# Issuing all of batch 0's loads ahead, smaller last chunks, and weights in quarters, in a fused attention and MLP kernel

## Chip, cores and metric

One core of a Trainium2 chip. The metric is the device time of one execution in microseconds (us), the median of several runs. A run lists its span, which is the part that the profile covers and some 1.8 us less than the time, and its mean granted TensorE clock (1.0 is full speed). All runs told here were in the same state (called fast). Differences of a few tenths of a microsecond are read from the traces, where single starts can be compared. A ratio of times is always the mean time of one kernel's fast runs over that of the other's fast runs of the same rounds, so it is not quite the ratio of the medians quoted beside it.

## The reference, cut to what matters

```python
B, N, C = 4, 6080, 256                       # d_ff = 2048
qn = q / (norm(q, axis=1) + 1e-6)            # norms over all N tokens
kn = k / (norm(k, axis=1) + 1e-6)
a  = softmax(kn.transpose(0, 2, 1) @ qn / tau)   # 256 x 256 for each batch
x  = v @ a                                   # 24320 x 256
out = gelu_tanh(x @ w_in) @ w_out
```

The norms and the 256 x 256 matrix need all tokens of q and k of a batch. For batch 0 nothing else can run meanwhile. For batches 1 to 3 that work is spread between the matmuls of the batch before.

## The kernel before

The kernel first computes G (k transposed times q) and the column sums of squares of batch 0, chunk by chunk. Then follow the softmax and aw = a @ w_in, folded so that a block of 512 tokens needs only v transposed, gelu, and w_out. The loads of batch 0 (cut):

```python
first_chunks = chunks_of([12, 12, 5, 6, 4, 4, 2, 2], 2)   # slots of 128 tokens
fillers = [0, 0, 5, 7, 4, 3, 1, 0]                        # filler matmuls before each chunk, results unused
def stage_chunk(n):          # takes a staging buffer of four: waits until an older chunk is used up
    ...
    load_chunk((nc.sync, nc.scalar if n < 1 else nc.sync), st, 0, first_chunks[n], 2)
for n in range(2):
    stage_chunk(n)
...
for n, ch in enumerate(first_chunks):
    # VectorE casts q and k to bf16, ScalarE squares them
    keep_clock(fillers[n])
    for s, rows in slots_of(ch, 128):
        gram(G, qkb, s, rows, seen == 0, seen == n_all - 1)
    # sums of the squares by matmuls with a column of ones
    for x in ((2, 3) if n == 0 else (4, 5) if n == 1 else (n + 4,)):
        stage_chunk(x)
```

The weights (cut). All casts and the loads of v go through POOL's queue, in this order:

```python
for half in range(2):
    # two DMAs of w_in, each cast on POOL
    load_v(1 + half)                          # POOL: block 1 and 2 of v
for half in range(2):
    w = flat_stage(8)
    nc.sync.dma_start(out=w, in_=wout_v[:, half * 8 : half * 8 + 8, :])      # rows of 1 KB
    nc.gpsimd.tensor_copy(wout_bf[:, half * 8 : half * 8 + 8, :], w)
```

```python
vT = vT_of.pop(nb)
turn_v(nb + 2)        # SP: four DMA transposes of the v block after next
load_v(nb + 3)        # POOL: load of a later v block
...                   # a few steps on, POOL: load_qk, first chunk of the next batch
```

## Time and profile before

| | |
|---|---|
| time | 754.13 us, median of 3 (753.9 to 754.29) |
| TensorE busy | 97% of a span of 752.0 us |
| column sums of batch 0 end | 35.95 us |
| first matmul of block 0, of block 1, of block 2 | 40.06, 52.26, 64.84 us |
| holes on TensorE after 40 us | one, 0.7 us, before the yp matmuls at 51.83 |

The profile's lines that carry this are shown in the prediction. A chain line has start, length and what. A window line has the stretch, its length, the busy time of TensorE, its weight loads, VectorE, ScalarE and POOL (each with its count), and then the granted clock, the DMA share and GB/s.

### The profile page before, as it was taken

To read this page: it belongs to the slowest core of one execution; us is meant where nothing else is said; L and a number is where in the kernel's file an instruction comes from. 1 tells how busy PE (TensorE), PEld (TensorE's weight loads), DVE (VectorE), ACT (ScalarE), POOL (GpSimd) and SP (SyncE) were. 2 spreads that over 40 slices of the span, in tenths; PEclk is the share of its full clock that TensorE was granted. 3 is DMA by queue.
4 is the path that set the end of the run, shared out by engine and by line. 5 is a ranking of instruction groups with operands and counts; after the bars stand their busy time and mean duration, and the time that the engine had idled before them with its cause. 6 is when DMAs were issued, how large, how long until landed. Compare 5 with 4: busy or idle time off the path is not lost.

```text
span 752.0 us, 12341 instructions
## 1 busy us (share of the span) xinstructions
PE 726.4 (97%) x5186; PEld 502.3 (67%) x5274; DVE 284.3 (38%) x497; ACT 420.3 (56%) x411; POOL 80.8 (11%) x154
## 2 busy tenths in 40 slices
PE   2899999999999999999999999999999999999998
PEld 1656766776666766776666666776666666666666
DVE  3733556463501646554521265555351011011011
ACT  4875555556456555555555555555645655555552
POOL 1061111101012102101001102010101000000000
PEclk9999999999999999999999999999999999999999
DMA  9989685613237685824325876671413533322111
GB/s 369 400 205 200 104 150 139 132 43 69 70 72 144 114 163 108 164 63 75 71 57 117 141 119 124 150 143 46 69 43 85 105 85 70 69 75 54 41 57 57
DMA packets 80183, 85.69 MB, mean 114 GB/s; under 512 B 55424, under 2 KB 59136, under 8 KB 79616
## 3 DMA queue, kind: packets, MB, share of 16 engines
q0 software_dynamic: 14480, 30.87, 25.7%
q1 hardware_dynamic: 65344, 52.39, 24.4%
q10 hardware_dynamic: 304, 1.64, 0.5%
q8 instruction: 41, 0.67, 0.4%
q14 instruction: 14, 0.11, 0.0%
HBM read 78.91 MB, written 24.90 MB: 138 GB/s over the span
## 4 chain that ended last, share of the span: by engine, by line
PE 94%; DMA 3%; ACT 1%; issue 1%; DVE 0%; POOL 0%; SPq 0%; DVEq 0%; POOLq 0%
PE yp L528 44%; PE hp L602 43%; PE G L158 4%; PE ps L218 2%; ACT sq L269 1%; DMA st<-in_q_dram 1%; DMA st<-in_k_dram 1%; PE T L196 0%; POOL wout_bf L359 0%; PE yp L633 0%; PE cols L170 0%; DVE qk L267 0%; DVE aw L413 0%; DVE Gs L188 0%; ACT eT L383 0%
## 5 line engine op out<-in xcount | busy, mean ns | idle before, releaser
L606 ACT ACTIVATE g<-hp 128x1024 bf16<-128x1024 f32 (+1 forms) x384 | 389.8, 1015 | 307.0 <-PE hp L602 295.2
L528 PE MATMUL yp<-wout_bf,g 128*128 128x256 bf16 x3024 | 392.0, 273 | 1.6 <-POOL wout_bf L359 0.7
L602 PE MATMUL hp<-vT,aw 128*128 128x512 bf16 (+1 forms) x1456 | 383.9, 377 | 3.8 <-DVE aw L413 0.2
L528 PEld LDWEIGHTS <-g 128*128 128x128 bf16 x3024 | 295.9, 98 | 114.3 <-issue 1.2
L602 PEld LDWEIGHTS <-aw 128*128 128x128 bf16 x1536 | 149.9, 98 | 104.1 <-DVE aw L413 0.5
L545 DVE COPY ysb<-yp 128x512 f32<-128x512 f32 (+1 forms) x95 | 64.9, 683 | 396.5 <-PE yp L528 396.5
L460 DVE TENSOR_TENSOR acc<-acc,sq 128x512 f32<-128x512 f32 x141 | 97.6, 692 | 4.8
L459 DVE TENSOR_TENSOR sq<-qkb 128x512 bf16<-128x512 bf16 x141 | 58.9, 418 | 0.0
L158 PE MATMUL G<-qkb 128*128 128x256 bf16 x288 | 55.0, 273 | 0.0
L307 POOL DMA_DIRECT2D vb<-in_v_dram x47 | 25.9, 552 | 88.6 <-DMA vT<-vb 81.3
L227 DVE TENSOR_SCALAR aw<-ps,rsinv 128x512 bf16<-128x512 f32 x30 | 22.4, 749 | 23.5 <-PE ps L218 18.3
L158 PEld LDWEIGHTS <-qkb 128*128 128x128 bf16 x288 | 28.2, 98 | 3.3
L332 POOL CAST gate<-g 1x1 f32<-1x1 bf16 x24 | 5.9, 245 | 227.8 <-ACT g L606 227.8
L158 PE MATMUL G<-qk 128*128 128x256 bf16 x96 | 13.5, 298 | 15.8 <-DVE qk L267 15.8
L269 ACT ACTIVATE sq<-st 128x3072 bf16<-128x3072 f32 (+2 forms) x9 | 21.1, 2379 | 11.1 <-DMA st<-in_q_dram 8.2
L158 PEld LDWEIGHTS <-qk 128*128 128x128 bf16 x96 | 9.8, 106 | 19.1 <-DVE qk L267 16.6
L267 DVE CAST qk<-st 128x3072 bf16<-128x3072 f32 (+2 forms) x10 | 14.2, 1438 | 13.1 <-DMA st<-in_q_dram 10.0
L218 PE MATMUL ps<-win_bf,eT 128*128 128x512 bf16 x54 | 16.4, 379 | 0.2
L479 POOL TENSOR_TENSOR r<-r,half 128x4 f32<-128x4 f32 x3 | 3.1, 1042 | 103.4 <-DVE r L478 103.4
L82 POOL DMA_DIRECT2D qkb<-in_q_dram x24 | 12.9, 537 | 5.8 <-issue 4.3
L585 POOL COPY g<-gr 128x1024 bf16<-128x1024 bf16 x2 | 2.1, 1036 | 101.3 <-PE yp L528 101.3
L82 POOL DMA_DIRECT2D qkb<-in_k_dram x24 | 12.9, 539 | 0.0
(73 smaller groups left out, 109.0 us busy)
## 6 DMA issues: line engine op xcount, KB each, us to landing
out_dram<-ysb SPq DMA_DIRECT2D x44, 512.0 KB, 3.0
vb<-in_v_dram POOLq DMA_DIRECT2D x43, 256.0 KB, 6.2
qkb<-in_q_dram POOLq DMA_DIRECT2D x21, 384.0 KB, 4.6
qkb<-in_k_dram POOLq DMA_DIRECT2D x21, 384.0 KB, 6.4
st<-in_q_dram SPq DMA_DIRECT2D x2, 1536.0 KB, 11.8
vT<-vb SPq DMA_TRANSPOSE x184, 3.0
wst<-in_moe_w_in_dram SPq DMA_DIRECT2D x4, 512.0 KB, 7.5
wst<-in_moe_w_out_dram SPq DMA_DIRECT2D x2, 1024.0 KB, 11.7
```

The costliest lines, as they stand in the source:

```text
L82: engines[x].dma_start(out=dst[x][:, 0:size, :], in_=src[b, s0 * 128 : (s0 + size) * 128, :].rearrange("(p s) c -> p s c", s=size))
L158: nc.tensor.matmul(G[:, ic, :], lhsT=qk[1][:rows, s, ic * 128 : ic * 128 + 128], rhs=qk[0][:rows, s, :], start=first and ic == 0, stop=las ...
L218: nc.tensor.matmul(ps, lhsT=eT[:, jc, ic * 128 : ic * 128 + 128], rhs=win_bf[:, jc, fs * 512 : fs * 512 + 512], start=jc == 0, stop=jc == 1)
L227: nc.vector.tensor_scalar_mul(dst, ps, scale)
L269: nc.scalar.activation(sq, x, AF.Square)
L307: nc.gpsimd.dma_start(out=t[:, 0:n, :], in_=v_rows[r0 : r0 + n * 128, :].rearrange("(p s) c -> p s c", s=n))
L459: nc.vector.tensor_mul(sq[:rows], flat, flat)
L460: nc.vector.tensor_add(acc[:rows], acc[:rows], sq[:rows])
L528: nc.tensor.matmul(yp[:rows, at, :], lhsT=g[:, fc, s * 128 : s * 128 + rows], rhs=wout_bf[:, fc, :], start=fc == 0, stop=fc == FC - 1)
L545: nc.vector.tensor_copy(ysb[:, s0 : s + 1, :], yp[:, 0 : s + 1 - s0, :])
L602: nc.tensor.matmul(hp[:, j, :cols], lhsT=aw[:, cc, fc * 128 : fc * 128 + 128], rhs=vT[:, cc, :cols], start=cc == 0, stop=cc == 1)
L606: nc.scalar.activation(g[:, 2 * i : 2 * i + 2, :cols], hp[:, :, :cols], AF.Gelu_apprx_tanh)
```

## The change

The intent: no load of batch 0 waits for a staging buffer, since idle buffers of later stages (g, aw) serve as homes; the last chunks are smaller, so that less work follows the last landing; w_out arrives in quarters with longer rows, so that its first users need not wait for a half; and the first exponentials begin when their own tile is ready. In the chunks numbered 6 and 7, POOL casts k and VectorE squares q (`CASTS_POOL`, `SQUARES_DVE`), which spreads the last work over more engines.

```diff
-    first_chunks = chunks_of([12, 12, 5, 6, 4, 4, 2, 2], 2)
-    fillers = [0, 0, 5, 7, 4, 3, 1, 0]
+    first_chunks = chunks_of([2, 12, 12, 5, 4, 4, 4, 2, 1, 1], 3)
+    fillers = [0, 0, 0, 5, 6, 5, 4, 2, 1, 0]
+    SQUARES_DVE = (6, 7)
+    CASTS_POOL = (6, 7)
...
+    staged = [
+        slot_pair(shared, 0, 2),
+        ([g[:, 0:12, :] for g in g_homes], None),
...
+    for n, ch in enumerate(first_chunks):
+        load_chunk((nc.sync, nc.scalar if n < 1 else nc.sync), staged[n][0], 0, ch, 2)
...
-    for half in range(2):
-        w = flat_stage(8)
-        nc.sync.dma_start(out=w, in_=wout_v[:, half * 8 : half * 8 + 8, :])
-        nc.gpsimd.tensor_copy(wout_bf[:, half * 8 : half * 8 + 8, :], w)
+    for fs in range(4):
+        w, T = w_quarter(), t_of(fs)
+        rows_of_w = moe_w_out[fs * 512 : fs * 512 + 512, :]
+        nc.sync.dma_start(out=w.rearrange("p (e t c) -> p e t c", t=T, c=256),
+                          in_=rows_of_w.rearrange("(e p t) c -> p e t c", p=128, t=T))
+        nc.gpsimd.tensor_copy(wout_bf[:, fs * 4 : fs * 4 + 4, :], w.rearrange("p (f c) -> p f c", c=256))
...
-    for cc in range(2):
-        p = pH.tile([128, 2, 512], FP32, tag="h", name="vps")[:, 0, :]
+    vps = pH.tile([128, 2, 512], FP32, tag="h", name="vps")
+    spare = pH.tile([128, 2, 512], FP32, tag="h", name="spare")
...
+    T = [pY.tile([128, 512], FP32, tag="y", name="T") for _ in range(2)]
```

Because a partition now holds four neighbouring rows of w_out, the columns of aw are stored in the matching order (the eviction reads PSUM with a stride). Cut here: the column order, the first quarter of w_in in two pieces, and the order of the first evictions of aw.

More of the change, by code (lines that the diff above doesn't have):

```diff
@@ L93 @@
     n_all = S_ALL + 1
-    first_chunks = chunks_of([12, 12, 5, 6, 4, 4, 2, 2], 2)
-    TAIL, SHARED = 4, 6
-    fillers = [0, 0, 5, 7, 4, 3, 1, 0]
-    staged = []
+    first_chunks = chunks_of([2, 12, 12, 5, 4, 4, 4, 2, 1, 1], 3)
+    n_chunks = len(first_chunks)
+    TAIL = 4
+    fillers = [0, 0, 0, 5, 6, 5, 4, 2, 1, 0]
+    SQUARES_DVE = (6, 7)
+    CASTS_POOL = (6, 7)
     def halves(pool, tag, dtype, size, most=SMAX):
@@ L107, in halves, with slot_pair @@
         return [t.rearrange("p a b c -> p (a b) c") for t in tiles], None
-    def stage_chunk(n):
-        if n < len(first_chunks):
-            _, size, rem = first_chunks[n]
-            if n < SHARED:
-                st, whole = halves(stage, "st", FP32, size)
-            else:
-                _, size, rem = first_chunks[n - 2]
-                whole = staged[n - 2][1][:, :, size + rem :, :]
-                st = [whole[:, x] for x in range(2)]
-                rem = False
-            if rem:
-                nc.gpsimd.memset(whole[:, :, size, :], 0.0)
-            load_chunk((nc.sync, nc.scalar if n < 1 else nc.sync), st, 0, first_chunks[n], 2)
-            staged.append((st, whole))
-    for n in range(2):
-        stage_chunk(n)
+    def slot_pair(whole, lo, hi):
+        return [whole[:, x, lo:hi, :] for x in range(2)], whole[:, :, lo:hi, :]
+    g_homes = [gp.tile([128, FC, 512], BF16, tag="g", name="g").bitcast(FP32) for _ in range(2)]
+    aw_homes = [awp.tile([128, 2, D], BF16, tag="aw", name="aw").bitcast(FP32).rearrange(
+        "p x (s c) -> p x s c", c=256) for _ in range(2)]
+    st_homes = [stage.tile([128, 2, SMAX, 256], FP32, tag="st", name="st") for _ in range(4)]
+    shared = st_homes[3]
+    staged = [
+        slot_pair(shared, 0, 2),
+        ([g[:, 0:12, :] for g in g_homes], None),
+        ([t.rearrange("p a b c -> p (a b) c") for t in st_homes[:2]], None),
+        slot_pair(st_homes[2], 0, 6),
+        slot_pair(aw_homes[0], 0, 4),
+        slot_pair(aw_homes[1], 0, 4),
+        ([g[:, 12:16, :] for g in g_homes], None),
+        slot_pair(shared, 2, 4),
+        slot_pair(shared, 4, 5),
+        slot_pair(shared, 5, 6),
+    ]
+    nc.gpsimd.memset(staged[3][1][:, :, 5, :], 0.0)
+    for n, ch in enumerate(first_chunks):
+        load_chunk((nc.sync, nc.scalar if n < 1 else nc.sync), staged[n][0], 0, ch, 2)
     ident = const.tile([128, 128], FP32)
@@ L147, with t_of, sorted_columns, pieces @@
     win_v = moe_w_in.rearrange("(c p) d -> p c d", p=128)
-    wout_v = moe_w_out.rearrange("(t p) d -> p t d", p=128)
+    def t_of(fs):
+        return 2 if fs == 0 else 4
+    def sorted_columns(ps, fs):
+        return ps.rearrange("a (e p t) -> a e t p", p=128, t=t_of(fs))
+    def pieces(dst, fs):
+        return dst.rearrange("a (e t p) -> a e t p", p=128, t=t_of(fs))
     def keep_clock(n, pool=pH, tag="h"):
@@ L199, in turned, with row_sums @@
         return T
-    def row_sums(eT):
-        rs = pA.tile([128, 512], FP32, tag="a", name="rs")
+    def row_sums(eT, rs=None):
+        if rs is None:
+            rs = pA.tile([128, 512], FP32, tag="a", name="rs")
         for ic in range(2):
@@ L212, in row_sums, with aw_part @@
         return rsinv
-    def aw_part(eT, rsinv, aw, fs, ic, ps=None, act=False):
+    def aw_part(eT, rsinv, aw, fs, ic, ps=None):
         if ps is None:
@@ L222, in aw_part @@
                 start=jc == 0, stop=jc == 1)
-        dst, scale = aw[:, ic, fs * 512 : fs * 512 + 512], rsinv[:, ic : ic + 1]
-        if act:
-            nc.scalar.activation(dst, ps, AF.Copy, scale=scale)
-        else:
-            nc.vector.tensor_scalar_mul(dst, ps, scale)
+        dst = pieces(aw[:, ic, fs * 512 : fs * 512 + 512], fs)
+        nc.vector.tensor_scalar_mul(dst, sorted_columns(ps, fs), rsinv[:, ic : ic + 1])
     G = pA.tile([128, 2, 256], FP32, tag="a", name="G")
     cols = pA.tile([128, 512], FP32, tag="a", name="cols")
-    n_chunks = len(first_chunks)
     seen, summed = 0, 0
@@ L265 @@
             todo = [[y[:, :, 0:hi] for y in (qk_whole, sq_whole, whole)]]
+        if n in CASTS_POOL:
+            nc.gpsimd.tensor_copy(qkb[1][:, 0:hi], st[1])
+            todo = [(qkb[0][:, 0:hi], None, st[0])]
         for to, sq, x in todo:
-            nc.vector.tensor_copy(to, x)
-            if n != n_chunks - 2:
-                nc.scalar.activation(sq, x, AF.Square)
-        if n == n_chunks - 2:
-            nc.scalar.activation(sqb[1][:, 0:hi], st[1][:, 0:hi], AF.Square)
+            nc.vector.tensor_copy(to[:, 0:hi] if whole is None else to, x)
+            if sq is not None and n not in SQUARES_DVE:
+                nc.scalar.activation(sq[:, 0:hi] if whole is None else sq, x, AF.Square)
+        if n in SQUARES_DVE:
+            nc.scalar.activation(sqb[1][:, 0:hi], st[1], AF.Square)
             nc.vector.tensor_mul(sqb[0][:, 0:hi], qkb[0][:, 0:hi], qkb[0][:, 0:hi])
@@ L279 @@
             waiting = None
-        if n < 2:
+        if n < 3:
             pairs_of(n, sqb)
@@ L285 @@
             sums_of([[y[:rows, s, :] for y in sqb] for s, rows in slots_of(ch, 128)], n == n_chunks - 1)
-        for x in ((2, 3) if n == 0 else (4, 5) if n == 1 else (n + 4,)):
-            stage_chunk(x)
     v0 = stage.tile([128, 2, SMAX, 256], FP32, tag="st", name="v0")
@@ L343, in load_qk, with w_quarter @@
             loaded_of[b, n] = views, t
-    def flat_stage(n):
-        w = stage.tile([128, 2, SMAX, 256], FP32, tag="st", name="wst")
-        return w.rearrange("p a b c -> p (a b c)")[:, 0:2048].rearrange("p (c d) -> p c d", c=n)
-    for half in range(2):
-        w = flat_stage(2)
-        for x in range(2):
-            c0 = half * 1024 + x * 512
-            nc.sync.dma_start(out=w[:, :, x * 512 : x * 512 + 512], in_=win_v[:, :, c0 : c0 + 512])
-            nc.gpsimd.tensor_copy(win_bf[:, :, c0 : c0 + 512], w[:, :, x * 512 : x * 512 + 512])
-        load_v(1 + half)
-    for half in range(2):
-        w = flat_stage(8)
-        nc.sync.dma_start(out=w, in_=wout_v[:, half * 8 : half * 8 + 8, :])
-        nc.gpsimd.tensor_copy(wout_bf[:, half * 8 : half * 8 + 8, :], w)
+    w_homes = []
+    def w_quarter():
+        n = len(w_homes)
+        if n % 3 == 0:
+            t = stage.tile([128, 2, SMAX, 256], FP32, tag="st", name="wst")
+            t = t.rearrange("p a b c -> p (a b c)")
+        else:
+            t = w_homes[-1]
+        w_homes.append(t)
+        return t[:, n % 3 * 1024 : n % 3 * 1024 + 1024]
+    for fs in range(4):
+        w = w_quarter().rearrange("p (c d) -> p c d", c=2)
+        step = 256 if fs == 0 else 512
+        for lo in range(0, 512, step):
+            c0 = fs * 512 + lo
+            nc.sync.dma_start(out=w[:, :, lo : lo + step], in_=win_v[:, :, c0 : c0 + step])
+            nc.gpsimd.tensor_copy(win_bf[:, :, c0 : c0 + step], w[:, :, lo : lo + step])
+        if fs % 2:
+            load_v(1 + fs // 2)
+    for fs in range(4):
+        w, T = w_quarter(), t_of(fs)
[3 more added lines that the diff above has]
+        nc.gpsimd.tensor_copy(wout_bf[:, fs * 4 : fs * 4 + 4, :], w.rearrange("p (f c) -> p f c", c=256))
     r = smx.tile([128, 4], FP32, tag="r", name="r")
@@ L366, with turn_v0 @@
     Gs = scaled(G, r)
-    vps = []
-    for cc in range(2):
-        p = pH.tile([128, 2, 512], FP32, tag="h", name="vps")[:, 0, :]
+    vps = pH.tile([128, 2, 512], FP32, tag="h", name="vps")
+    spare = pH.tile([128, 2, 512], FP32, tag="h", name="spare")
+    def turn_v0(cc):
         for s in range(4):
-            nc.tensor.matmul(p[:, s * 128 : s * 128 + 128],
+            nc.tensor.matmul(vps[:, cc, s * 128 : s * 128 + 128],
                              lhsT=v0[:, s, cc * 128 : cc * 128 + 128],
                              rhs=ident, is_transpose=True)
-        vps.append(p)
-    keep_clock(1, pY, "y")
-    T = turned(Gs)
-    keep_clock(1, pY, "y")
+    turn_v0(0)
+    T = [pY.tile([128, 512], FP32, tag="y", name="T") for _ in range(2)]
+    for ic in range(2):
+        for jc in range(2):
+            nc.tensor.matmul(T[jc][:, ic * 128 : ic * 128 + 128],
+                             lhsT=Gs[:, ic, jc * 128 : jc * 128 + 128],
+                             rhs=ident, is_transpose=True)
+    turn_v0(1)
     vT0 = vts.tile([128, 2, 512], BF16, tag="vT", name="vT")
-    nc.vector.tensor_copy(vT0[:, 0, :], vps[0])
+    nc.vector.tensor_copy(vT0[:, 0, :], vps[:, 0, :])
     eT = smx.tile([128, 2, 256], BF16, tag="eT", name="eT")
@@ L382, with first_aw @@
     for jc in range(2):
-        nc.scalar.activation(eT[:, jc, :], T[:, jc, :], AF.Exp, scale=r[:, jc : jc + 1])
-    nc.scalar.activation(vT0[:, 1, :], vps[1], AF.Copy)
+        nc.scalar.activation(eT[:, jc, :], T[jc][:, 0:256], AF.Exp, scale=r[:, jc : jc + 1])
+    nc.scalar.activation(vT0[:, 1, :], vps[:, 1, :], AF.Copy)
     firsts = []
-    def first_aw(n, jc, pool=pY, tag="y"):
+    def first_aw(n, jc, pool=pA, tag="a"):
         if jc == 0:
@@ L400 @@
     first_aw(1, 0)
-    rsinv = row_sums(eT)
+    rsinv = row_sums(eT, spare[:, 0, :])
     first_aw(0, 1)
@@ L404 @@
     for n in (2, 3):
-        first_aw(n, 0, pA, "a")
+        first_aw(n, 0, pY, "y")
         first_aw(n, 1)
-    for n in range(4):
+    for n, t, act in ((0, 0, False), (1, 0, True), (0, 1, True), (1, 1, False), (2, None, False), (3, None, False)):
         ic, lo = n % 2, n // 2 * 256
-        dst, scale = aw[:, ic, lo : lo + 256], rsinv[:, ic : ic + 1]
-        if n == 1:
-            nc.scalar.activation(dst, firsts[n][:, 0:256], AF.Copy, scale=scale)
+        dst = aw[:, ic, lo : lo + 256].rearrange("a (t p) -> a t p", t=2)
+        ps = firsts[n][:, 0:256].rearrange("a (p t) -> a t p", t=2)
+        if t is not None:
+            dst, ps = dst[:, t], ps[:, t]
+        scale = rsinv[:, ic : ic + 1]
+        if act:
+            nc.scalar.activation(dst, ps, AF.Copy, scale=scale)
         else:
-            nc.vector.tensor_scalar_mul(dst, firsts[n][:, 0:256], scale)
+            nc.vector.tensor_scalar_mul(dst, ps, scale)
     nc.scalar.activation(dummy, ones_f, AF.Gelu_apprx_tanh)
-    aw_left = [(fs, ic, *((pA, "a") if fs == 2 else (pY, "y"))) for fs in range(1, 4) for ic in range(2)]
+    aw_left = [(fs, ic, *((pY, "y") if fs == 2 else (pA, "a"))) for fs in range(1, 4) for ic in range(2)]
     def more_aw(n):
```

## The prediction

> **What bounds the kernel now.** I read the summary of the page first, then the chain that ended last, in order of time, then the timeline and the windows of the stretch in which TensorE is not yet full.
>
> ```profile
> span 752.0 us, 12341 instructions
> PE 726.4 (97%) x5186; PEld 502.3 (67%) x5274; DVE 284.3 (38%) x497; ACT 420.3 (56%) x411; POOL 80.8 (11%) x154
> PE 94%; DMA 3%; ACT 1%; issue 1%; DVE 0%; POOL 0%; SPq 0%; DVEq 0%; POOLq 0%
> ```
>
> TensorE is busy 97% of the span and is 94% of the chain. All of the diff acts before some 52 us: it touches the loads and reductions of batch 0, its softmax and the weights. What follows is matmuls back to back whose number does not change. So the question is only by how much sooner the full stretch begins, and whether a hole near its start closes. The chain shows the start:
>
> ```profile
> 0.73 10.15 DMA st<-in_q_dram
> 10.90 7.42 ACT sq L269 x3
> ...
> 18.88 2.76 ACT sq L269
> 22.02 9.55 DMA st<-in_k_dram
> 31.66 1.24 DVE qk L267
> 32.95 1.05 PE G L158 x8
> ```
>
> Columns are start, length and what. It looks like DMA, then ScalarE (which frees a buffer), then DMA again. The windows say that the middle link is no real gap: the transfers never paused (the last two figures are DMA share and GB/s).
>
> ```profile
> 5.00:10.00 5.00, 0.00 (x0) 0.00 (x0) 0.00 (x0) 0.00 (x0) 0.00 (x0) 1.00 1.01 430
> 10.00:15.00 5.00, 0.61 (x3) 0.43 (x4) 4.10 (x3) 4.10 (x2) 1.07 (x1) 1.00 1.02 433
> 15.00:20.00 5.00, 4.47 (x46) 3.39 (x44) 3.85 (x4) 5.00 (x3) 0.00 (x0) 1.00 0.98 407
> 20.00:25.00 5.00, 4.22 (x52) 3.44 (x54) 4.14 (x4) 4.39 (x2) 0.00 (x0) 1.00 1.02 410
> 25.00:30.00 5.00, 5.00 (x51) 3.62 (x50) 3.34 (x4) 3.66 (x2) 0.00 (x0) 1.00 1.02 404
> ```
>
> From 5 to 30 us the share is 0.98 to 1.02 throughout. The wait for a buffer delayed the issue of a chunk (13.69, 16.34, 19.04, 21.65 us), but there was always older work in the queue. Issuing all at once therefore buys almost no transfer time. After the last landing comes a serial tail, also from the chain:
>
> ```profile
> 35.76 0.19 PE cols L170 x8
> 35.98 0.18 ACT r L363
> 37.30 0.75 PE T L196 x4
> 38.08 0.48 ACT eT L383
> 39.24 0.18 DVE rsinv L211
> 39.52 0.50 DVE aw L413
> 40.06 1.04 PE hp L602 x4
> 49.91 1.88 POOL wout_bf L359
> 51.83 0.60 PE yp L528 x4
> ```
>
> Column sums end at 35.95, the first block matmul starts at 40.06, and at 51.83 TensorE has waited 0.71 us for a cast of half of w_out (the waits view: L528 <- POOL wout_bf L359, 0.7). These three places are all that the change can win.
>
> [...] from 12 to 15 us only the SP queue was moving data, at 442 GB/s, no less than the 430 of both queues. [...] in the trace the first exponential starts at 38.08, after the last of the four transposes into its bank (38.05)[...]
>
> **Loads.** The bytes stay (6080 x 256 x 4 B x 2 = 12.45 MB); the row lengths change. From the packet records of the trace, median time of one packet on the SP queue: 12 KB rows 460 ns, 6 KB 238, 5 KB 200, 4 KB 162, 2 KB 86, 1 KB 46. One slot (128 tokens of q and k) is 16 KB for each of the 16 engines, so it costs 0.61 us in 12 KB rows, 0.64 in 5 or 6 KB, 0.65 in 4 KB, 0.69 in 2 KB, 0.74 in 1 KB. Before: 24 slots x 0.61 + 5 x 0.64 + 0.37 (the remainder) + 6 x 0.635 + 8 x 0.65 + 4 x 0.69 = 30.05 us. After: 24 x 0.61 + 5 x 0.64 + 0.37 + 12 x 0.65 + 4 x 0.69 + 2 x 0.74 = 30.3. So the last chunk lands about **0.27 us later**. Before, it landed at about 34.15 (issued near 25.6, the two small k loads taking 9.3 us to land in the median), so after at about 34.4. The instruction order of the changed kernel also shows that "all at once" is really eight SP transfers ahead: from the ninth on, an issue waits for an earlier landing. With some 18 slots in flight that never starves the engines.
>
> **Tail of the loads.** The last chunk has one slot, not two. Its cast is about 0.4 us (0.69 for 1024 elements before) and its square 0.61 (the row of 512 elements), against 1.06 before. Counted from the landing alone, the sums would end at 34.4 + 0.1 + 0.6 + 0.2 = 35.3. But TensorE has its own queue of work. The last eight slots cost 16 Gram matmuls at 0.107 to 0.13 us, 32 column sums at 0.024, and the fillers ahead of the last three chunks, now 2 + 1 + 0 at 0.21: some 1.8 + 0.8 + 0.6 = 3.2 us, in order. They start once the four-slot chunk is ready: it lands at about 34.4 - 2 x 0.69 - 2 x 0.74 = 31.6, and its half cast on POOL takes 1.04 (the win_bf row of the same size), so 32.7. That ends at 35.9, and before it was 35.95. I take a gain of **0.1 us** here, between zero and 0.6: the new fillers eat most of what the smaller chunk wins.
>
> **Softmax of batch 0.** The root, the norms and the scaling of G are unchanged. The four transposes now write two banks, so the first exponential may start after the third transpose, some 0.15 us sooner. The transposes of v's second half move behind T (four in 0.5 us), beside the exponentials. The first eviction of aw has pieces of 128 columns, so the first pair of block matmuls waits for about 0.35 us rather than 0.50 (estimate: 0.479 for 256 columns[...]). Together **0.3 us**. The strided read of PSUM is in the later batches too, but an eviction (0.75 us) comes there once per slot of some 2 us, off the path.
>
> **Weights.** Before, w_out came in two halves of 1 KB rows, landing near 45.9 and 49.8, with casts of 1.90 us each. Now four quarters, three in 4 KB rows: 16 x 0.086 + 3 x 8 x 0.162 = 5.3 us of packets per engine rather than 128 x 0.046 = 5.9, and casts of 1.04. Adding up the queue after 34.4: v0 1.3, w_in 5.6, the v blocks of POOL 2.75, the first three quarters 4.0: the third lands at 48.0 to 48.6 and is cast by 49.7; it is first read near 50.5. The fourth has until 51.9 and is cast near 51. So the hole of **0.7 us** closes.
>
> Sum: 0.1 + 0.3 + 0.7 = 1.1 to 1.2 us off 754.13: **752.9 us**.
>
> **Rivals.** (1) The load phase really is shortened: if the waits for buffers starved some DMA engines, 1 to 2 us come off and the time is 751 to 752. Against it: the share of 0.98 to 1.02. For it: the rate falls from 433 to 407 at 15 us, while 12 KB rows were still in flight. (2) The tail is bound by TensorE or POOL rather than by the landing: if the casts on POOL collide with VectorE's copies, or the fillers come late, the sums end 0.3 to 0.8 us later than before and the time is 753.3 to 754. For it: the chain is nearly gapless on TensorE from 32.95 on. (3) The hole at w_out is passed on: w_in's first quarter in 1 KB rows or the later quarters arrive too late, the wait turns up at another line, and the time stays at 753.6 to 754.1. Against it: nearly 1 us of slack by the sums above.
>
> **Range and chances.** If (1) holds beside my gains I get 751.5; if (2) and (3) hold together, 754.1. Repeated runs differ by 0.4 us. So 751.6 to 754.1. Two per cent would be 15 us, about half of the whole load phase, in either direction; nothing in the diff can reach that.
>
> **What would show it.** Right: DMA share near 1.0 up to 34 us as before, the last q or k landing at 34 to 34.7; column sums ending at 35.4 to 36.1; first block matmul at about 39.6; no wait of the yp matmuls for wout_bf and a TensorE busy time that has hardly changed. Wrong: a first block matmul before 38.5 (rival 1), or after 40.2 (rival 2); a wait of yp or ps for a weight cast above 0.3 us (rival 3); or a slower full stretch after 60 us, which would mean that the strided evictions or the new layout cost TensorE time after all.

Where a cut is marked, the forecast spoke of the hardware beyond what a trace of this case shows. No term of its sum is lost by that: it stays 0.1 + 0.3 + 0.7 = 1.1 (to 1.2) us off 754.13, so 752.9. For the load phase, the argument is the DMA share of 0.98 to 1.02. The 0.35 us for a piece of 128 columns stands as an estimate from the trace before, in which an eviction of 256 columns took 0.479 us and one of 512 took 0.750, so that one of 128 comes to about 0.34. That casts on POOL and work on VectorE hinder each other (rival 2) was a supposition; what was measured is told below.

## The result, and the profile after

The changed kernel takes **754.5 us** (754.08 to 755.56, 4 runs) against 754.01 of before (753.6 to 754.29, 4 runs). The ratio is 1.0009, interval 0.9992 to 1.0026: the same. I had predicted 752.9 and a range up to 754.1.

The head of the page, after:

```profile
span 752.3 us, 12381 instructions
PE 728.3 (97%) x5195; PEld 503.5 (67%) x5283; DVE 285.3 (38%) x501; ACT 420.4 (56%) x414; POOL 82.5 (11%) x159
PE 90%; DMA 7%; SPq 1%; issue 1%; POOL 0%; DVE 0%
```

DMA's share of the chain has gone from 3% to 7%, which is the first sign. The chain in order of time, after, up to 66 us:

```profile
3.60 18.70 DMA st<-in_k_dram
...
23.17 9.84 DMA st<-in_k_dram
...
34.02 7.41 DMA wst<-in_moe_w_in_dram
41.43 0.05 issue
41.48 0.99 POOL win_bf L378
42.47 6.60 DMA vb<-in_v_dram
49.07 0.02 issue
49.08 1.30 SPq L335
...
53.05 11.92 DMA vT<-vb
64.97 0.14 issue
65.11 1.02 PE hp L639 x4
```

Before, the chain left the loads at 31.57 and ran through the engines from there, for the most part TensorE. Now it runs through the loads until 65.11: the weights, then v of block 2, then its DMA transposes, the last of which takes 11.92 us to land. The matmuls of block 2 wait for it. The windows of the two kernels beside each other, first before and then after:

```profile
50.00:55.00 5.00, 4.29 (x29) 2.55 (x27) 0.00 (x0) 2.97 (x4) 4.94 (x8) 1.00 0.54 81
60.00:70.00 10.00, 9.95 (x70) 6.67 (x69) 3.35 (x6) 6.16 (x7) 1.36 (x3) 1.00 1.12 221
```

```profile
50.00:55.00 5.00, 5.00 (x35) 3.23 (x33) 0.00 (x0) 3.84 (x4) 3.81 (x9) 1.00 0.82 118
60.00:70.00 10.00, 9.12 (x62) 5.90 (x62) 3.35 (x6) 5.25 (x6) 1.43 (x3) 1.00 1.24 137
```

TensorE (the first busy time) gains 0.71 us from 50 to 55, where the hole at w_out was, and loses 0.83 from 60 to 70. The waits of TensorE say the same. Columns: who waited for whom, us in total, times, longest. Before, then after:

```profile
PE yp L528 <- POOL wout_bf L359: 0.7, 1, 0.7
```

```profile
PE hp L639 <- DMA vT<-vb: 0.8, 1, 0.8
```

Why do the transposes land late? The timeline of POOL shows when it issued v of block 3 and the first chunk of batch 1. Before, then after:

```profile
51.72 0.54 POOL L307 DMA_DIRECT2D vb<-in_v_dram  x1
52.95 0.54 POOL L82 DMA_DIRECT2D qkb<-in_q_dram  x1
```

```profile
49.96 0.54 POOL L321 DMA_DIRECT2D vb<-in_v_dram  x1
51.19 0.54 POOL L82 DMA_DIRECT2D qkb<-in_q_dram  x1
```

POOL finishes the casts of w_out 1.76 us sooner, and so its next loads go out 1.76 us sooner, into the stretch in which SP issues the transposes (from 48.90 before, from 49.08 after). By the landing records of the traces, the four transposes of block 2 landed at 51.3, 52.6, 57.6 and 61.5 before, and at 53.2, 56.4, 60.1 and 65.0 after: the first two, issued ahead of POOL's next load, 1.3 us apart before, and all four 3.2 to 4.8 apart with POOL's loads among them after. The view of the transposes' line has 8.6 us from issue to landing before and 12.6 after, but that is the median of 12 transposes of three blocks: it is 8.4 in the sixth experiment and 9.1 in the tenth, though block 2 waits in the sixth alone. So the landings of block 2 itself are compared here. From the issue of its first transpose to the landing of its fourth it takes 12.6 us before and 15.9 after.

The front did not gain either. The root, which follows the column sums, starts at 36.26 instead of 35.98. From there to the matmuls after block 0's first pair it takes 4.88 us (to 41.14) instead of 4.95 (to 40.93).

### The profile page after: what moved, and what is told of

It reads as the page before. It is cut to its first block, busy times and chain, and to the rows that moved or that the text cites. A ratio compares the mean times of both kernels' runs of the same rounds, so it can differ in the third digit from the quotient of the medians.

```text
span 752.3 us, 12381 instructions
## 1 busy us (share of the span) xinstructions
PE 728.3 (97%) x5195; PEld 503.5 (67%) x5283; DVE 285.3 (38%) x501; ACT 420.4 (56%) x414; POOL 82.5 (11%) x159
## 4 chain that ended last, share of the span: by engine, by line
PE 90%; DMA 7%; SPq 1%; issue 1%; POOL 0%; DVE 0%
PE yp L565 43%; PE hp L639 41%; PE G L176 4%; DMA st<-in_k_dram 4%; DMA vT<-vb 2%; PE ps L237 1%; DMA wst<-in_moe_w_in_dram 1%; DMA vb<-in_v_dram 1%; SPq L335 1%; SPq L82 0%; PE yp L670 0%; PE T L214 0%; POOL win_bf L378 0%; SPq L377 0%; PE cols L188 0%
## 5 line engine op out<-in xcount | busy, mean ns | idle before, releaser
L496 DVE TENSOR_TENSOR sq<-qkb 128x512 bf16<-128x512 bf16 x141 | 58.9, 418 | 0.0
L176 PEld LDWEIGHTS <-qk 128*128 128x128 bf16 x96 | 10.3, 111 | 17.7 <-DVE qk L285 14.1
L82 POOL DMA_DIRECT2D qkb<-in_q_dram x24 | 12.9, 537 | 5.7 <-issue 4.1
L287 ACT ACTIVATE sq<-st 128x3072 bf16<-128x3072 f32 (+2 forms) x6 | 10.6, 1769 | 5.0 <-DMA st<-in_k_dram 2.8
L82 POOL DMA_DIRECT2D qkb<-in_k_dram x24 | 12.9, 538 | 0.0
L657 POOL COPY gr<-g 128x1024 bf16<-128x1024 bf16 x2 | 2.1, 1036 | 81.6 <-ACT g L643 81.6
```

The lines of the kernel that those rows point to most:

```text
L82: engines[x].dma_start(out=dst[x][:, 0:size, :], in_=src[b, s0 * 128 : (s0 + size) * 128, :].rearrange("(p s) c -> p s c", s=size))
L176: nc.tensor.matmul(G[:, ic, :], lhsT=qk[1][:rows, s, ic * 128 : ic * 128 + 128], rhs=qk[0][:rows, s, :], start=first and ic == 0, stop=las ...
L287: nc.scalar.activation(sq[:, 0:hi] if whole is None else sq, x, AF.Square)
L496: nc.vector.tensor_mul(sq[:rows], flat, flat)
```

## Experiments

Theory A: the hole at w_out was closed, and the gain was handed on to block 2, because POOL is free sooner, loads sooner, and delays the transposes. Rival B: the new load phase delays everything. Rival C: the transposes are late for another reason. Theory D: a part of the loss is the clock, which stands at half (0.50) for some microseconds of the load phase in some runs. "Held" means that POOL's loads are held back.

One table for all runs. Block 1 and block 2 are the starts of their first matmuls in the profiled run, in us, and the gap is their difference. It is 12.6 where nothing waits. From block 2 to the end of the span it takes 687.1 to 687.5 us in every row except the first experiment (689.0), so the start of block 2 decides the time.

| kernel | block 1 | block 2 | gap | span of this run, its clock | median time, us | before, same rounds |
|---|---|---|---|---|---|---|
| before | 52.26 | 64.84 | 12.6 | 752.0, 1.0 | 754.13 | |
| changed | 51.53 | 65.11 | 13.6 | 752.3, 1.0 | 754.5 | 754.01 |
| 1 new weights only | 51.31 | 67.27 | 16.0 | 756.3, 0.998 | 755.72 | 754.12 |
| 2 old weights | 52.63 | 65.22 | 12.6 | 752.6, 1.0 | 754.96 | 754.12 |
| 3 POOL loads held | 54.86 | 67.45 | 12.6 | 754.6, 0.995 | 755.94 | 754.12 |
| 4 v of block 0 apart | 53.03 | 66.82 | 13.8 | 754.0, 0.998 | 754.72 | 754.12 |
| 5 new weights only, held | 52.93 | 65.52 | 12.6 | 753.0, 0.997 | 753.83 | 754.18 |
| 6 fillers moved | 51.22 | 64.25 | 13.0 | 751.4, 1.0 | 753.30 | 754.18 |
| 7 no late fillers | 52.77 | 67.04 | 14.3 | 754.2, 0.998 | 756.39 | 754.18 |
| 8 casts on VectorE | 53.13 | 65.72 | 12.6 | 752.9, 0.997 | 755.42 | 754.18 |
| 9 fillers moved, old weights | 52.82 | 65.40 | 12.6 | 752.8, 1.0 | 754.68 | 754.11 |
| 10 fillers moved, loads held | 50.84 | 63.42 | 12.6 | 750.6, 1.0 | 752.58 | 754.11 |
| 11 as 10, and 4 and 8 | 50.88 | 63.46 | 12.6 | 750.6, 0.999 | 752.57 | 754.11 |
| 12 before, fillers moved | 52.97 | 65.55 | 12.6 | 752.7, 0.999 | 754.05 | 754.11 |

All gave the right result.

### 1. The kernel before with the new weights only

```diff
-    for half in range(2):  ... w_in in halves, w_out in halves
+    for fs in range(4):    ... w_in and w_out in quarters, columns of aw sorted, as in the change
```

> The kernel before with only the weights part of the change (quarters, 4 KB rows of w_out, sorted columns); loads and softmax as before. Theory A (the closed hole at w_out is handed to block 2, whose transposed v lands late because the POOL queue is free sooner and issues the next loads sooner): no wait of yp for a w_out cast, the column sums end at 35.9 to 36.1 and the first block matmul is at about 40.1 as before, the loads for v block 3 and batch 1 are issued at about 50 and 51.2 instead of 51.7 and 53.0, the last transpose of v for block 2 lands near 65 instead of 61.6, block 2's first matmuls wait 0.8 to 1.2 us for it, and the time is within 0.3 us of before. Rival B (it is the new load phase and softmax that cost the time and delay the transposes): block 2 does not wait, and the time is 0.6 to 0.9 us below before.

The hole is gone (block 1 starts 0.95 us sooner than before). POOL's loads went out at 50.22 and 51.45, and block 2 waited. The wait in this profile was 3.2 us, far more than I had expected. The median is 755.72 (ratio 1.0015, 1.0002 to 1.0029), not "within 0.3 of before" but worse. The timeline and the windows of TensorE show why the loss is larger than the wait:

```profile
67.27 1.87 PE L620 MATMUL hp<-vT,aw 128*128 128x512 bf16 x4 [3.21 <-DMA vT<-vb]
```

```profile
65.00:70.00 5.00, 2.73 (x10) 1.35 (x10) 2.44 (x5) 0.74 (x1) 0.00 (x0) 0.72 1.20 152
```

After 3.2 idle us the four matmuls take 1.87 us instead of 1.03, and the granted clock of the stretch is 0.72: by the trace's clock record it is half from 67.22 to 70.63. Rival B falls: the load phase here is the old one, and block 2 waits all the same.

### 2. The changed kernel with the old weights

```diff
-    for fs in range(4):    ... quarters, sorted columns
+    for half in range(2):  ... halves, unsorted, as before
```

> The changed kernel with the weights loaded as before (halves, 1 KB rows of w_out, columns unsorted), everything else changed. Theory A: the wait of yp for the second w_out cast is back at 0.5 to 0.9 us, the POOL loads are issued at about 51.8 and 53 again, the last transpose for block 2 lands near 62 and nothing waits for it; the time is 0.1 to 0.4 us above before, because the front (sums and softmax) is 0.2 us later. Rival B: block 2 still waits for its transposes by 0.5 us or more and the time is 0.8 us or more above before.

As theory A has it. The waits of TensorE show the old hole and no wait for transposes:

```profile
PE G L178 <- DVE qk L287: 1.5, 1, 1.5
PE yp L555 <- POOL wout_bf L376: 0.9, 1, 0.9
PE T L397 <- DVE Gs L208: 0.8, 1, 0.8
```

The profiled span, at a clock of 1.0, is 752.6. The median of 754.96 is higher than expected, because three of the five runs had a clock of 0.995 to 0.997 and spans of 753.1 to 754.4. Of the nine runs of the kernel before in the same rounds, one had 0.997 and one 0.998. That was the first hint of theory D.

### 3. The changed kernel with POOL's loads held back

```diff
-            if n in (3, 9):
-                load_qk(b, n // 6)
+            if b == 1 and n == 6:
+                pace()              # POOL waits for activation 6 of block 0
+                load_v(3)
+            if n in ((7, 9) if b == 1 else (3, 9)):
+                load_qk(b, n // 8 if b == 1 else n // 6)
...
-            load_v(nb + 3)
+            if nb > 0:
+                load_v(nb + 3)
```

> The changed kernel, but the POOL loads of v block 3 and of the first chunk of batch 1 are held back until the sixth and seventh activation of block 0, so that they are issued near 51.3 and 52.6, about as before. Theory A: the last transpose for block 2 lands at 61.5 to 63.5, the wait of block 2 for it (0.83 us in the changed kernel) is gone, TensorE runs without a hole from 41 us on, and the span is 0.8 to 1.1 us below the changed kernel's 752.3, near 751.4: 0.5 to 0.7 us faster than before. Rival C (the transposes are late for another reason, such as their own issue or the write of the weights): the wait stays at 0.5 us or more and the time is that of the changed kernel.

The wait for the transposes is gone (gap 12.6). The fourth lands 8.6 us after the first was issued, instead of 15.9. All of block 0 came late in this run, so the loads were issued at 54.54 and 56.48 and not at the expected 51.3 and 52.6. But the time rose to 755.94 (ratio 1.002, 1.0008 to 1.0033), and all five runs had a clock of 0.995 to 0.998. The windows of the load phase:

```profile
20.00:25.00 5.00, 3.80 (x18) 2.70 (x19) 4.63 (x4) 4.07 (x2) 0.00 (x0) 0.51 1.03 408
25.00:30.00 5.00, 4.92 (x51) 3.53 (x50) 3.22 (x4) 4.58 (x3) 0.00 (x0) 0.80 1.02 404
```

From 20 to 27 us TensorE ran at half clock. Its matmuls fell behind the loads, and with the fillers between them it never caught up: block 0 started at 43.44. Block 0 was thus 3.3 us late and the span only 2.3 longer than the changed kernel's, so 1.0 came back, which is the wait. This profile supports A but cannot show the gain.

What differs from the changed kernel's own profile is the idle time just before the Gram matmuls of the 12-slot chunk that starts near 21 us. The same line in the third experiment:

```profile
21.20 5.30 PE L176 MATMUL G<-qk 128*128 128x256 bf16 x24 [2.62 <-DVE qk L285]
```

and in the changed kernel:

```profile
20.95 2.79 PE L176 MATMUL G<-qk 128*128 128x256 bf16 x24 [1.50 <-DVE qk L285]
```

Over the profiled runs up to the eighth, idle times of 1.24 (before), 1.47 and 1.50 us were followed by full clock, and 1.61, 1.84, 1.90 and 2.62 by half clock (the eighth, half clock, 1.8).

### 4. v of block 0 in separate PSUM tiles

```diff
-            nc.tensor.matmul(vps[:, cc, s * 128 : s * 128 + 128],
+            nc.tensor.matmul((vps, spare)[cc][:, 0, s * 128 : s * 128 + 128],
-    nc.scalar.activation(vT0[:, 1, :], vps[:, 1, :], AF.Copy)
+    nc.scalar.activation(vT0[:, 1, :], spare[:, 0, :], AF.Copy)
-    rsinv = row_sums(eT, spare[:, 0, :])
+    rsinv = row_sums(eT, vps[:, 1, :])
```

> The changed kernel with the two halves of the transposed v of block 0 in separate PSUM tiles, so that VectorE's copy of the first half need not wait for the transposes of the second. Expected if the single tile is what swallowed the softmax gain: that copy starts at 37.9 instead of 38.80, the copy on ScalarE ends near 39.7 instead of 40.13, ScalarE's aw pieces start by 39.75 instead of 40.02, and the first block's four matmuls end 0.25 to 0.4 us sooner. The total does not move (within 0.2 us of the changed kernel), because block 2 then waits 0.25 to 0.4 us longer for its transposes. If the tile is not the cause, the first block's matmuls stay where they are.

The half clock fell on this run's load phase too (sums 1.66 us late), so only differences count. From the root to the matmuls after block 0's first pair it is 4.72 us instead of 4.88 (37.92 to 42.64). The tile cost 0.16 us, less than the 0.25 to 0.4 I had given it. Block 2's gap is 13.8: what comes before it is swallowed by the wait, as expected.

### 5. New weights only, with POOL's loads held

```diff
 # the first experiment's kernel, and
+                pace(); load_v(3)    # and load_qk at step 7, as in the third experiment
```

> The kernel before with the new weights (as the first experiment) and the POOL loads held back until activations 6 and 7 of block 0; loads and softmax of before. It tests the wait for the transposes without the new load phase, whose clock spoiled the profile of the held version of the changed kernel. Theory A: the last transpose for block 2 lands by 62.5, no matmul waits for it, the closed hole at w_out stays won, the span is 751.0 to 751.4 where the granted clock is 1.0, and the time is 0.6 to 0.9 us below before. Rival C (the transposes are late for another reason): the wait of 1 to 3 us of the first experiment stays and the time is 1 us above before.

With the old load phase, holding the loads takes the wait away: no wait of TensorE after 42 us, gap 12.6. Block 1 started 1.6 us later than in the first experiment, which alone gives the transposes more time, but they also landed sooner: at 52.0, 53.3, 57.4 and 58.9, against 53.2, 56.0, 61.9 and 67.1 in the first experiment. The median falls from 755.72 to 753.83, 0.35 below before (ratio 0.9996, 0.9984 to 1.0009). The two runs whose clock rounds to 0.999 or 1.0 and that had the shortest spans had 751.4 and 751.5; the others, with clocks down to 0.997, 752.0 to 753.0. Rival C falls. The expected 0.6 to 0.9 was not reached in the median, and the profiled run had half clock from 21 to 25 us.

### 6. The changed kernel with its fillers moved

```diff
-    fillers = [0, 0, 0, 5, 6, 5, 4, 2, 1, 0]
+    fillers = [0, 0, 8, 0, 2, 5, 3, 0, 0, 0]
```

> The changed kernel with the filler matmuls moved: eight before the third chunk, where TensorE idled for 1.5 us (2.6 us in the held version, after which it ran at half clock for 5.8 us), and 2, 5, 3 and none before the later ones. Theory D (part of the time lost is the clock, which falls when the idle stretch between the second and third chunk is long enough, so that TensorE runs late into the softmax): no stretch of half clock between 20 and 45 us, all five runs with a mean clock of 1.0 and spans within 0.4 us of each other, column sums ending at 35.5 to 35.8, the time 0.2 to 0.6 us below the changed kernel's. Rival E (the clock in the load phase does not follow from the idle stretch): runs with a clock of 0.995 and spans of 753.5 and more still occur, as in two of four runs of the changed kernel that lie below 1.0.

As theory D has it. All five runs have a clock of 1.0 and spans of 751.3 to 752.3 (a spread of 1.0, not 0.4). The median is 753.30: 1.2 below the changed kernel and 0.9 below before. The ratio of 0.9991 has an interval of 0.9978 to 1.0003, so it just includes no difference. The root starts at 35.70. Rival E falls. But the edit did two things at once: it filled the idle time before the third chunk, and it took the 2 + 1 fillers away from the last chunks. Between the two profiled runs, both at a clock of 1.0, the 0.9 us of span come from the second (root 0.56 us sooner) and from a shorter wait for the transposes (0.28 instead of 0.83), less some 0.2 lost elsewhere, and not from the clock; what the clock adds is seen in the slower runs of the changed kernel (752.8 and 753.8).

### 7. No fillers before the last chunks

```diff
-    fillers = [0, 0, 0, 5, 6, 5, 4, 2, 1, 0]
+    fillers = [0, 0, 0, 5, 6, 5, 4, 0, 0, 0]
```

> The changed kernel without the 2 + 1 fillers ahead of the last chunks. If TensorE's own queue is what ends the load phase, as the prediction said, the column sums end 0.5 to 0.65 us sooner relative to the moment when the four-slot chunk is ready (3.4 us after it in the changed kernel, 2.75 to 2.9 here) as long as the clock is 1.0; if the landing bounds it, less than 0.2 us sooner. The total does not follow (within 0.3 us of the changed kernel), since block 2 waits for its transposes.

From the start of the four-slot chunk's Gram matmuls to the last column sums it is 2.69 us (34.50 to 37.19), against 3.34 in the changed kernel (32.88 to 36.22): 0.65 less, which is what three fillers of 0.21 cost. Here the matmuls began after the last landing (34.44), but the sixth experiment, on time and at full clock, gives the same: 2.70 us (32.96 to 35.66). So with these casts the tail is set by TensorE's own queue. The total was worse than expected (756.39), with half clock from 21 us in the profiled run, clocks of 0.995 to 0.998 in all four, and 1.5 us of waiting for the transposes. Two effects are mixed there, and I draw nothing from the total.

### 8. The casts of k back on VectorE

```diff
-    CASTS_POOL = (6, 7)
+    CASTS_POOL = ()
```

> The changed kernel with the two casts of k back on VectorE (squares split as changed). If the move to POOL costs more than it wins (its 1.04 us cast of 1024 elements against 0.69 on VectorE, and VectorE's own cast of 512 elements taking 0.76 us beside it against 0.43 alone), the Gram matmuls of the four-slot chunk start 0.2 to 0.4 us sooner, at 32.5 to 32.7, VectorE's cast of 512 elements is back at 0.43, and the sums end 0.2 to 0.4 us sooner. If the move wins, they start later than 32.9.

Inconclusive by itself: half clock from 21 us made TensorE late (the four-slot chunk's matmuls at 34.49), so the cast was not what they waited for. The eleventh run answers it. This run also has an exception to theory A: POOL's loads went out as soon after the first transpose as in the changed kernel (0.87 us), and yet the fourth transpose landed at 61.84, only 11.9 us after the first was issued. With block 2 not needing it before 65.72, nothing waited.

### 9. Fillers moved, old weights

```diff
 # the second experiment's kernel, and
+    fillers = [0, 0, 8, 0, 2, 5, 3, 0, 0, 0]
```

> The changed kernel with the fillers moved (as in the sixth experiment) but the weights loaded as before: the new loads and softmax under a steady clock, without the new weights. All runs at a mean clock of 1.0. The first block's matmuls start at 39.4 to 39.7 as in the sixth experiment, against 40.06 before; the wait of yp for the second w_out cast is back at 0.8 to 1.2 us; block 2 waits for no transpose. Theory A with D: spans of 751.6 to 752.0, 0.2 to 0.5 us above the sixth experiment and 0.1 to 0.5 below before. If the new weights won nothing of their own, the span is that of the sixth experiment, 751.4.

This expectation missed. The clock was 1.0 in all six runs and block 0 started at 39.36, 0.7 us sooner than before, but the time is 754.68: nothing of it was left. TensorE's waits:

```profile
PE yp L555 <- POOL wout_bf L376: 1.7, 1, 1.7
```

The hole at w_out grew from 0.7 to 1.7 us. With the old halves, the second cast waited for its load to land (3.38 us of POOL's time here, and 3.37 in the twelfth experiment; before, the landing was at 49.83 and the cast began at 49.88), so it holds block 1 at about 52.3 to 53.0 in every profile with the old halves (before, experiments 2, 9 and 12), whatever comes before. A faster front alone is worth nothing.

### 10. Fillers moved, and POOL's loads held

```diff
 # the third experiment's kernel, and
+    fillers = [0, 0, 8, 0, 2, 5, 3, 0, 0, 0]
```

> The changed kernel with the fillers moved and the POOL loads held back: no wait for w_out, no wait of block 2 for transposes (0.3 us in the sixth experiment's profile), clock 1.0 in all runs. Theory A with D: spans of 750.9 to 751.3, the time 0.1 to 0.5 us below the sixth experiment's and 1.0 to 1.4 below before, which is what I had predicted for the change. Against it: holding the loads makes batch 1's first chunk late and a Gram matmul waits for it; the time then is above the sixth experiment's.

**752.58 us** against 754.11 (ratio 0.9985, 0.9971 to 0.9998); four of the five runs have a clock of 1.0 and spans of 750.6 to 750.8. All that TensorE still waits for after 20 us:

```profile
PE G L176 <- DVE qk L285: 1.5, 3, 0.7
PE G L176 <- POOL qk L282: 0.3, 1, 0.3
PE vps L399 <- DMA v<-in_v_dram: 0.3, 1, 0.3
PE T L407 <- DVE Gs L206: 0.3, 1, 0.3
PE hp L643 <- ACT aw L448: 0.2, 1, 0.2
```

No wait is left for w_out or for the transposes. This is 0.2% below the kernel before, in the same rounds; the changed kernel ran in other rounds, with a median of 754.5. Of the 0.8 us of span between the profiles of the sixth experiment and this one, 0.45 is the shorter gap; 0.38 was there before block 1 began, which the held loads do not explain.

### 11. All repairs

```diff
 # the tenth, and separate tiles for v of block 0 (experiment 4), and
-    CASTS_POOL = (6, 7)
+    CASTS_POOL = ()
```

> As the tenth, and also the two halves of v of block 0 in separate PSUM tiles and the casts of k back on VectorE. The separate tiles gave 0.16 us between the root and the second group of matmuls; the casts should let the four-slot chunk start 0.2 to 0.4 us sooner and the sums end 0.1 to 0.3 us sooner, unless the landing bounds them by then (last landing at 34.46). Expected: spans of 750.5 to 751.0, 0.2 to 0.5 us below the tenth. If POOL's casts were free, no difference from the tenth beyond 0.15 us.

No gain over the tenth: 752.57 (ratio 0.9989, 0.997 to 1.0009). One of six runs took 757.08, unexplained (clock 0.998; only the first run's trace is at hand). The four-slot chunk's matmuls do start 0.41 us sooner (32.41 against 32.82), but then TensorE waits between the last chunks, and the sums end at the same time (35.56 against 35.54). There the landings bound it: the last one is at 34.48, and ScalarE squares that chunk until 35.22, just before the last sums at 35.32. Separate tiles are not worth keeping for time.

### 12. The kernel before with its fillers moved

```diff
-    fillers = [0, 0, 5, 7, 4, 3, 1, 0]
+    fillers = [0, 6, 0, 6, 3, 4, 0, 0]
```

> The kernel before with only its fillers moved: six before the second chunk, none before the third, then 6, 3, 4, none, none. It tells whether the gain of moved fillers belongs to the change or was open before it. Theory D: clock 1.0 in all runs (two of nine runs of the kernel before had 0.997), the sums end at 35.7 to 35.9 instead of 35.95 (one filler less in the tail), and the time is 0.0 to 0.4 us below before; so at most 0.4 of the 0.9 us of the sixth experiment come from the fillers alone. If it is 0.8 us or more below before, the fillers are the whole gain and the change has no part in it.

754.05 against 754.11 (ratio 0.9999, 0.9985 to 1.0013): no gain. The sums ended at 36.49, 0.55 us later than before and at full clock, so this placing of the fillers made the front worse (block 0 started at 40.61), and the wait for w_out is 0.9 us. With the old halves a sooner front would not have shown either, as the ninth experiment has it. So moved fillers alone give nothing with the old weights; this one placing says no more.

## Why the prediction was wrong

**The step that failed** is in the first part: "All of the diff acts before some 52 us" and "These three places are all that the change can win." From it followed the sum, in which a hole closed at 52 us was taken for time won at the end. The runs show a third gate behind it, the transposes of block 2, which had 3.3 us of slack before (landed at 61.5, needed at 64.84) and which the change itself delayed by 3.4 us through POOL's earlier loads.

The experiments show it: with the new weights and no holding the gap is 13.0 to 16.0 us (changed kernel, 1, 4, 6 and 7), with holding it is 12.6 (3, 5, 10 and 11). The landings say it without the gap. Where POOL's load of v left 2.8 to 4.2 us after the first transpose of block 2 (before, 2, 3, 5, 9 and 12), the fourth landed 8.6 to 13.8 us after the first was issued. Where it left 0.85 to 0.88 us after it (changed kernel, 1, 4, 6 and 7), the fourth landed after 14.1 to 17.8. The eighth experiment, also at 0.87, is the exception (11.9, no wait), so the delay is not the same in each run. In the tenth and eleventh v's load left at about 1.0 us and only the first chunk of batch 1 clearly later (2.8 to 3.0 instead of 2.1); the fourth landed after 12.9 and 13.3. Which of the two loads does the harm was not tested apart. Rival 3 had the right form ("the hole at w_out is passed on"), but looked for the wait at the weights.

Point by point:

- **Loads.** Right. By the landing records the last chunk landed at 34.47 (predicted 34.4), 0.19 us later than before (34.28), where I had 0.27, and the DMA share stayed at 0.99 to 1.07 from 5 to 35 us. Two slips of mine change nothing: the slot costs as printed sum to 29.98 and 30.25, not 30.05 and 30.3 (their difference, 0.27, stands), and nine transfers, not eight, left SP's queue before an issue had to wait for a landing (the tenth, at 8.02, after a landing at 8.00).
- **Tail of the loads.** The mechanism was right and the size off. TensorE's own queue took 3.34 us from the four-slot chunk on, against my 3.2, and began at 32.88 instead of 32.7. The root thus started 0.28 us later than before, where I had a gain of 0.1. Experiment 7 gives the fillers their 0.65 us.
- **Softmax.** Mis-sized: 0.07 us instead of 0.3, counted to the end of the first pair. To the first block matmul alone the gain was 0.24 (3.84 us after the root instead of 4.08); the second of the pair then waited 0.2 for ScalarE's piece of aw. (VectorE's first piece, of 128 columns, took 0.35 us, as estimated.) The hidden term was the copy of v. As both halves share one tile, VectorE's copy started at 38.80, after all of its transposes, and ScalarE's copy and its piece of aw followed late; separate tiles returned 0.16.
- **Weights.** Right in outcome. The hole of 0.7 us closed, and block 1 started 0.73 us sooner although the front was 0.2 later. But the third quarter landed at 46.52, not at 48.0 to 48.6, and POOL ended its last cast at 50.01, not near 51. So POOL was free for its next loads even sooner than my own sums said.
- **Rival 2** (the sums end later) came true twice. In the profiled run, at full clock, the sums ended 0.28 us later than before, by the fillers, which it had named. And in a form that I had not named: in two of the changed kernel's four runs the mean clock was 0.997 and 0.995, and their spans were 752.8 and 753.8 instead of 752.3 and 752.6. In the variants that keep the changed kernel's filler placing before the third chunk (experiments 2, 3, 4, 7 and 8) 20 of 22 runs were below 0.999; with eight fillers there (6, 9, 10 and 11) one of 22 was; of the kernel before, four of the 19 runs in the experiments' rounds. Where a profile of such a run was taken, it had half clock near 21 to 27 us. That the two slower runs of the changed kernel had it in the same place is likely, but no trace of them shows it.

Where the expected gain went, in the changed kernel's profile: the front gave 0.2 away, the closed hole brought about 0.9 (block 1 is 0.73 sooner with a front that is 0.2 later), and the wait for the transposes took 1.0 (gap 13.6 instead of 12.6). Together 0.3 us slower, which is the difference of the two spans (752.3 and 752.0). With the loads held and the fillers moved (experiment 10) the changed kernel is 1.5 us below before. That this is a little more than the 1.2 that I had promised is luck: about 0.6 of it comes from fillers that I had counted as a cost.

**What the clock records add.** Each trace holds a list of granted clocks with their times. In all 14 lists every stretch between two steps is 3.41 us long or a whole multiple of it (half clock from 67.22 to 70.63 in the first experiment; 733.87 us of full clock in the two kernels' own profiles, 215 times 3.4133), and the first step up to full clock falls anywhere between 16.7 and 19.4 us (17.93 before, 19.08 in the changed kernel, where the two lists begin and up to which the windows print 1.00; in the profile of before, the Gram matmuls of the first 12-slot chunk start 0.21 us apart up to the step and 0.11 after it). The idle time before the second 12-slot chunk lies, wholly or for the most part, in the 3.41 us that follow this step. Where TensorE was busy for 1.51 to 1.94 us of them (experiments 3, 4, 5, 7 and 8), half clock followed at their end; where it was busy for 1.91 to 3.36 (the other nine), it did not (busy times summed from the TensorE records of each trace). The two groups touch at 1.9; without the short matmuls of the column sums they part (0.93 to 1.36 against 1.54 to 3.21). Experiments 5 and 10 had the step at the same time, 17.59: with 1.94 busy us half clock followed, with 3.02 (fillers) it did not. So with as much as 1.94 us of work among the idle times the clock still fell. That the same kernel falls in some runs only because the step moves is my reading, and was not shown.

An early step also makes the idle time longer, since the matmuls of the first 12-slot chunk end sooner (the 24 took 4.21 us in the third experiment, 5.30 in the second): in the kernels with the changed load phase and no fillers there, it is 1.47 us for a step at 19.43 (the second) and 2.62 for one at 16.73 (the third). This is a pattern of 14 traces; only the filling of the idle time was tested.

**What stays open.** What sets the time of the first step is not shown. Why the wait in the first experiment was 3.2 us and 0.8 in the changed kernel is open as well.

**What was measured of shared engines.** In the kernel before, the loads moved 442 GB/s from 12 to 15 us, with one queue at work, and 430 from 5 to 10, with two. In the changed kernel a cast of 512 elements on VectorE took 0.76 us while POOL's cast ran beside it (from 32.34, POOL from 31.78 to 32.82), and 0.41 and 0.43 later, alone. The slow cast ended 0.28 us after POOL's, in less than the 0.41 that it takes alone, so VectorE was not held for the whole of POOL's cast. What POOL's earlier loads would meet I had asked for the load phase alone; the stretch after 48 us needed the same question.

## What to carry to other kernels

When a hole closes, follow the next few users of the same engines: ask for each queue what it will issue sooner, and what slack the transfers had that it meets. Several gates in series, each with small slack, make every single repair look useless (9, 12 and the change itself), so open them together before judging one. And fillers belong where TensorE would idle, not in front of a chunk whose data is already there: here, eight before the third chunk in the changed load phase went with one of 22 runs below a mean clock of 0.999, none there with 20 of 22, and three before the last chunks cost 0.65 us.
